# Sparse attention and a two-layer MLP on one core: the order of the first loads and the filler products at the start

## The chip, the core and the metric

The kernel runs on one core of a Trainium2 chip. A core has five engines that each work through an instruction stream of their own: TensorE (PE, the matrix products; its weight loads are listed apart as PEld), VectorE (DVE), ScalarE (ACT), GpSimd (POOL) and SyncE (SP). DMAs are issued from the streams of SP, ACT and POOL and travel on queues that belong to the issuing engine. The metric is the device time in microseconds (us) of one launch; lower is better. Several runs are made and the median is taken.

## The reference

The computation is a block of sparse attention followed by a two-layer network. q, k and v are float32 of shape 8 x 8 x 576 x 64 (batch, head, sequence, head dimension).

```
scores = scale * q @ k^T                                   # per batch and head
mask   = local  (0 <= row-col < 32)                        # heads 0 to 3
       | strided (row >= col and row % 32 == col % 32)     # heads 4 to 7
attn   = softmax(where(mask, scores, -1e9)) @ v
x      = attn, heads side by side: (8*576) x 512
h      = x @ w_in                                          # 512 -> 2048
g      = max(h, 0) + alpha * min(h, 0)
out    = g @ w_out                                         # 2048 -> 512, float32
```

## The kernel before

The heads of one batch make two units: the four local heads and the four strided heads. Unit 0 is local and unit 1 strided for batch 0, units 2 and 3 are those of batch 1, and so on. Two heads form a pair, and a pair's work is cut into pieces: `T` transposes q or k of a unit on TensorE (line 248) and copies the result to SBUF; `Sc` makes scores (L350), adds the mask with one more product (L366) and takes the exponential on ScalarE (L371, L374); `Pv` multiplies by v (L451), and VectorE divides by the row sums (L458, L460); `X` transposes the attention output into `xT` (L468).

The network takes 512 rows of x at a time. `lin1_piece` multiplies by w_in (L633), followed by a ReLU on ScalarE (L643) and an add on VectorE (L646); `lin2_piece` (L660), or `lin2_sums` from the third block on (L750), multiplies by w_out. There are nine such blocks. Attention of batch 0 runs alone at the start; everything after it interleaves attention pieces of later batches with the network's pieces.

Nothing is planned at run time: every call is wrapped in `keep`, and each engine executes its own instructions in the order in which the program emits them. That order matters most at the start, in the code from line 811 on:

- `load_qk(0, True, "q")` and `load_qk(0, True, "k")` (L123) load q and k of the four strided heads of batch 0, 512 KB each in float32. q goes by SP's queue and k by ACT's. Between the two calls the identity matrix, the first 128 columns of `consts` (32 KB), is issued on SP (L825). The rest of `consts` (90 KB, the masks, L832) and alpha (L833) follow on SP.
- VectorE has memsets: `wrm`, which the filler products read (L820), the padding of two buffers (L822) and of `x16s` (L823), then more (L842 to L845).
- POOL issues, in this order, the strided tails (`tl`, L158), the local q and k of batch 0 (`ql`, `kl`, L123), the local tails (L162), v for the strided heads (`stv`, L172), v for the local heads (`vl`, L180), then the four chunks of w_in (L801), of w_out (L797) and the loads of batch 1.
- `warm(n)` (L805) emits n filler products of 128x128 by 128x512 into a bank that nobody reads (L808). Twelve come first; then, in the loop over the pieces of batch 0, eight stand behind piece 0 (the transposes of q), three behind piece 1 (the transposes of k and of the tails), and one behind many of the later pieces.
- `id16` (L862) copies a corner of the identity; it needs the identity to have landed. Then `cast_s` casts q to float16, both halves on VectorE, and k, one half on VectorE (L190) and one on ScalarE (L188). `madd` (L865) makes the additive mask from the second part of `consts`.
- Piece 0 then transposes q, and copies its two halves from PSUM to `qT`, the first on VectorE (L190) and the second on ScalarE (L188). Piece 1 transposes k (one half copied on ScalarE, one on VectorE) and the tails (L273).
- At piece 4, VectorE casts v of the strided heads (`vs`).

Of the kernel before, what the change touches and what calls it, by code (L numbers as in the profile page):

```python
# [31 lines left out]
def kernel(  # L32
# [10 lines left out]
    nc = tc.nc  # L43
    keep = tc.keep_in_program_order
# [55 lines left out]
    x16s = cpool.tile([80, 1024], F16)  # L100
    qks = {nm: cpool.tile([80, 4, 512], F16, name=f"{nm}sd") for nm in "qk"}
# [5 lines left out]
    def load_qk(b, strided, nm):  # L107

        h0 = 4 if strided else 0
        src = q if nm == "q" else k
        if strided and b:
            t16 = hpool.tile([128, 2, 512], F16, tag=f"{nm}s", bufs=2, name=f"{nm}s")
            cast16[(b, True, nm)] = t16
        else:
            t16 = hpool.tile([128, 2, 512], F32, tag=f"{nm}l", bufs=2, name=f"{nm}l")
            loaded[(b, strided, nm)] = t16
        base = src[b, h0 : h0 + 1, 0:1, :]
        eng = nc.sync if (b > 2 and not strided) or (b == 0 and strided) else nc.gpsimd  # L120
        if b == 0 and strided and nm == "k":
            eng = nc.scalar
        keep(eng.dma_start(t16, bass.AP(  # L123
            tensor=base.tensor, offset=base.offset,
            ap=[[8 * D, 64], [2 * S * D, 2], [S * D, 2], [1, 8 * D]])))
# [13 lines left out]
    def cast_s(b, nm, eng):  # L139
        t16 = hpool.tile([128, 2, 512], F16, tag=f"{nm}s", bufs=2, name=f"{nm}s")  # L140
        if eng[0] == eng[1]:
            cast_copy(eng[0], t16, loaded[(b, True, nm)])
        else:
            for f in range(2):
                cast_copy(eng[f], t16[:, f : f + 1, :], loaded[(b, True, nm)][:, f : f + 1, :])
        cast16[(b, True, nm)] = t16
# [39 lines left out]
    def cast_copy(eng, o, i):  # L186
        if eng == "act":
            keep(nc.scalar.copy(o, i))  # L188
        elif eng == "dve":
            keep(nc.vector.tensor_copy(o, i))  # L190
        else:
            keep(nc.gpsimd.tensor_copy(o, i))

    def cast_v(b, pr, eng):

        v16 = vss[b % 2]
        cast_copy(eng, v16[0:72, 2 * pr : 2 * pr + 2, :, 0:64],
                  loaded[b][0:72, 1024 * pr : 1024 * pr + 1024].rearrange(
                      "p (h t d) -> p h t d", h=2, t=8))
        cast16[(b, True, "v")] = v16  # L200
# [338 lines left out]
    for g in range(7, npair + 2):  # L539
# [30 lines left out]
        for i, (kind, fn) in enumerate(seq):  # L570
# [6 lines left out]
            def run(fn=fn, extra=extra, g=g, c=c, kind=kind, lastp=(i == lastP), first=(i == 0)):  # L577
                fn()
                for b, pr in extra:
                    if pr in ("q", "k"):  # L580
                        cast_l(b, pr)
                        if b + 1 < B:
                            load_qk(b + 1, False, pr)
                        continue
                    cast_v(b, pr, "pool")
                    if pr == 1 and b + 1 < B:
                        load_v(b + 1, True)
                if kind == "Tk" and g % 4 == 3 and c + 3 < B:
                    load_tail(c + 3, False)
                if lastp:  # L590
                    if 4 * DX <= g - 1 < npair and pairs[g - 1].xd:
                        x_dma(pairs[g - 1])
                    if g % 4 == 3 and DX <= c + 1 < B:
                        transpose_d()
                    if g % 4 == 2 and DX <= c and c + 1 < B:
                        load_d(c + 1)
                    if g % 4 == 1 and DX < c and c + 1 < B:
                        load_v(c + 1, False)
                if first and 4 * DX <= g - 3 < npair and pairs[g - 3].xd and pairs[g - 3].strided:
                    x_copy(pairs[g - 3])  # L600
# [10 lines left out]
    def attn_step(end):  # L611
        if pos["i"] < end:
            pieces[pos["i"]][1]()
            pos["i"] += 1
        while late:
            late.pop(0)()
        if defer:
            defer.pop(0)()
# [186 lines left out]
    def warm(n):  # L805

        for _ in range(n):
            keep(nc.tensor.matmul(wps, wrm[:, 0:128], wrm, start=True, stop=True))  # L808


    wrm = gsum[0].rearrange("p k c -> p (k c)")[:, 0:512]
    wps = banks[2]
    def load_unit(b, strided, v_too=True):
        load_qk(b, strided, "q")
        load_qk(b, strided, "k")
        load_tail(b, strided)
        if v_too:
            load_v(b, strided)

    keep(nc.vector.memset(wrm, 0.0))  # L820
    for nm in "qk":
        keep(nc.vector.memset(qks[nm][64:80], 0.0))  # L822
    keep(nc.vector.memset(x16s[64:80], 0.0))  # L823
    load_qk(0, True, "q")
    keep(nc.sync.dma_start(consts[:, 0:128], consts_dram[:, 0:128]))  # L825
    load_qk(0, True, "k")
# [2 lines left out]
            name=nc.get_next_instruction_name(), act_func_set_id=6, ins=[], outs=[]  # L829
        )  # L830
    ))
    keep(nc.sync.dma_start(consts[:, 128:488], consts_dram[:, 128:488]))  # L832
    keep(nc.sync.dma_start(alpha_r, moe_alpha.rearrange("(kf p) -> kf p", p=128)))  # L833
    load_tail(0, True)
# [25 lines left out]

    warm(12)
    keep(nc.vector.tensor_copy(id16, ident[0:16, 0:16]))  # L862
    cast_s(0, "q", ("dve", "dve"))
    cast_s(0, "k", ("dve", "act"))
    keep(nc.vector.tensor_scalar(  # L865
        madd, consts[:, 128:488], -1.0, 30000.0, op0=ALU.add, op1=ALU.mult))
# [1 line left out]
    for i in range(end0):  # L868
        if i == 6:
            keep(nc.tensor.transpose(apt[:, 0:16], alpha_r, id16))  # L870
            keep(nc.vector.tensor_scalar(
                oma, apt[:, 0:16], -1.0, 1.0, op0=ALU.mult, op1=ALU.add))
        if i == 4:
            cast_v(0, 0, "dve")
            cast_v(0, 1, "dve")
        attn_step(end0)
        if i < 2:
            warm((8, 3)[i])
        elif i not in (2, 3, 4, 5, 11, 12, 14, 16):
            warm(1)  # L880

# [90 lines left out]
```

## Time and profile before

| quantity | value |
|---|---|
| median of 7 runs | 316.08 us (314.43 to 316.84) |
| time of the profiled execution | 316.84 us |
| span of the profiled execution, first to last instruction | 315.0 us |
| PE busy | 302.7 us, 96% of the span |
| DVE / ACT / POOL busy | 221.1 / 178.5 / 168.4 us |
| first `lin1_piece` product begins | 26.90 us |
| first score product begins | 13.71 us |
| mean DMA rate | 128 GB/s over the span |

In the rows below, a line of the timeline gives the start and the duration in us, the engine, the line of the kernel, the operation, what it writes and reads, how many were merged, and in brackets how long the engine stood idle before it and what ended that wait. "SPq" and "ACTq" are DMAs being issued by those engines. The chain is the list of work that ended last, followed backward from the end: for each piece its start, its length and what it was.

### The profile page before, as it was taken

How to read it: one execution, taken by the hardware profiler on the slowest of the kernel's cores; microseconds unless marked ns; L12 is line 12 of the kernel's file. 1: busy time of each engine (PE TensorE's matmuls, PEld its weight loads, DVE VectorE, ACT ScalarE, POOL GpSimd, SP SyncE). 2: the span in 40 equal slices, each digit the busy share in tenths (PEclk: the TensorE clock that was granted, in tenths of full speed). 3: DMA queues.
4: the chain of work that ended last, by engine and by line, in shares of the span. 5: the costliest groups of instructions: out<-in, count | busy, mean ns of one | idle time of the engine just before them, and what ended most of it. 6: DMA issues, size and time to landing. Idle time of an engine off the chain costs nothing.

```text
span 315.0 us, 7067 instructions
## 1 busy us (share of the span) xinstructions
PE 302.7 (96%) x2808; PEld 193.8 (62%) x2808; DVE 221.1 (70%) x408; ACT 178.5 (57%) x331; POOL 168.4 (53%) x175
## 2 busy tenths in 40 slices
PE   5999989999999999999999999999999999999995
PEld 1465445554454448844888888448844784585484
DVE  4466888457823789578856885689568967855872
ACT  2375645469566776476647754775467426615630
POOL 8672399235969773967396729672726301201300
PEclk9799999999999999999999999999999999999999
DMA  7999999999699992899699929963920040002003
GB/s 226 185 206 207 212 208 181 186 140 248 127 144 161 255 94 31 120 280 127 61 184 255 93 45 177 156 60 50 173 85 6 16 123 33 2 33 102 0 3 133
DMA packets 81202, 40.38 MB, mean 128 GB/s; under 512 B 58625, under 2 KB 76305, under 8 KB 81169
## 3 DMA queue, kind: packets, MB, share of 16 engines
q0 software_dynamic: 41728, 17.38, 50.2%
q1 hardware_dynamic: 39168, 22.03, 31.1%
q10 hardware_dynamic: 272, 0.52, 0.5%
q8 instruction: 22, 0.36, 0.5%
q14 instruction: 12, 0.09, 0.1%
HBM read 38.01 MB, written 9.44 MB: 151 GB/s over the span
## 4 chain that ended last, share of the span: by engine, by line
PE 64%; DVE 14%; ACT 8%; issue 4%; POOL 4%; DMA 4%; SPq 0%; ACTq 0%; DVEq 0%
PE hb L633 25%; PE hb L750 20%; PE hb L660 6%; DVE gT L646 6%; PE pv L451 3%; DVE x L460 2%; ACT neg L643 2%; PE tp L248 2%; DMA kl<-in_k_dram 2%; DVE wsum L690 2%; PE hb L808 2%; DMA consts<-consts 2%; ACT xT L490 2%; ACT et L421 2%; PE sp L408 1%
## 5 line engine op out<-in xcount | busy, mean ns | idle before, releaser
L646 DVE SCALAR_TENSOR_TENSOR gT<-neg,oma,hb 128x512 f16<-128x512 f32 x144 | 105.3, 744 | 40.4 <-ACT neg L643 33.7
L633 PE MATMUL hb<-xT,win 128*128 128x512 f16 (+1 forms) x640 | 132.9, 358 | 0.7
L643 ACT ACTIVATE neg<-hb 128x512 f32<-128x512 f32 x144 | 86.0, 597 | 39.2 <-PE hb L633 37.8
L633 PEld LDWEIGHTS <-win 128*128 128x128 f16 x640 | 60.1, 98 | 56.3 <-issue 2.6
L423 POOL TENSOR_TENSOR et<-et,consts 128x576 f16<-128x576 f16 (+1 forms) x24 | 30.6, 1276 | 54.4 <-ACT et L421 50.9
L702 POOL TENSOR_TENSOR gsum<-gT 128x512 f16<-128x512 f16 x21 | 24.2, 1150 | 50.6 <-DVE gT L646 50.6
L750 PEld LDWEIGHTS <-gsum 128*128 128x128 f16 x448 | 41.3, 98 | 5.9 <-DVE gsum L702 1.1
L750 PEld LDWEIGHTS <-gT 128*128 128x128 f16 x336 | 31.4, 98 | 6.8 <-DVE gT L646 1.8
L460 DVE TENSOR_TENSOR x<-pv,rc 96x384 f16<-96x384 f32 (+2 forms) x62 | 33.0, 532 | 2.1
L660 PE MATMUL hb<-wout,gT 128*128 128x512 f16 x128 | 32.5, 379 | 0.6 <-ACT osb L665 0.5
L430 POOL TENSOR_TENSOR et<-et,consts 128x576 f16<-128x576 f16 (+1 forms) x24 | 30.6, 1276 | 0.6 <-ACT et L427 0.6
L762 ACT COPY o<-hb 128x512 f32<-128x512 f32 (+1 forms) x28 | 15.8, 564 | 26.4 <-PE hb L750 26.4
L451 PEld LDWEIGHTS <-et 72*128 72x128 f16 (+1 forms) x448 | 23.7, 98 | 9.4 <-POOL et L430 0.9
L750 PE MATMUL hb<-wout,gT 128*128 128x256 f16 x216 | 28.0, 273 | 0.7 <-DVE gT L646 0.4
L458 DVE RECIPROCAL rc<-pv 72x6 f32<-72x6 f32 (+2 forms) x80 | 14.6, 183 | 19.0 <-PE pv L451 18.6
L750 PE MATMUL hb<-wout,gsum 128*128 128x256 f16 x216 | 26.9, 273 | 0.2 <-DVE gsum L702 0.2
L750 PE MATMUL hb<-wsum,gsum 128*128 128x256 f16 x216 | 26.3, 272 | 0.2 <-DVE gsum L702 0.2
L421 ACT ACTIVATE et<-sp 128x576 f16<-128x576 f32 (+1 forms) x24 | 15.5, 645 | 19.2 <-PE sp L408 19.2
L765 DVE TENSOR_TENSOR o<-hb,o 128x512 f32<-128x512 f32 (+1 forms) x21 | 14.2, 677 | 14.3 <-PE hb L750 10.6
L427 ACT ACTIVATE et<-sph 128x288 f16<-128x288 f32 (+1 forms) x48 | 18.4, 410 | 0.0
L188 ACT COPY qT<-tp 128x1024 f16<-128x1024 f16 (+1 forms) x11 | 8.9, 819 | 15.4 <-DVE qT L190 10.1
L660 PEld LDWEIGHTS <-gT 128*128 128x128 f16 x128 | 11.0, 97 | 9.8 <-issue 0.7
(104 smaller groups left out, 337.0 us busy)
## 6 DMA issues: line engine op xcount, KB each, us to landing
out_dram<-o SPq DMA_DIRECT2D x27, 256.0 KB, 3.0
ql<-in_q_dram SPq DMA_DIRECT2D x6, 512.0 KB, 6.1
kl<-in_k_dram SPq DMA_DIRECT2D x5, 512.0 KB, 7.0
stv<-in_v_dram POOLq DMA_DIRECT2D x8, 288.0 KB, 6.6
vl<-in_v_dram POOLq DMA_DIRECT2D x6, 384.0 KB, 8.2
win<-in_moe_w_in_dram POOLq DMA_DIRECT2D x4, 512.0 KB, 11.3
wout<-in_moe_w_out_dram POOLq DMA_DIRECT2D x4, 512.0 KB, 13.2
out_dram<-osb SPq DMA_DIRECT2D x8, 256.0 KB, 5.4
```

The source lines that it names most:

```text
L421: keep(nc.scalar.activation(ev.rearrange("r (y c) -> r y c", y=2), sp[0:r, :, 0:n], AF.Exp, scale=SCALE))
L423: keep(nc.gpsimd.tensor_tensor(mv, mv, m, op=ALU.mult))
L427: keep(nc.scalar.activation(ev[:, n * y : n * y + n], sps[y][0:r, 0:n], AF.Exp, scale=SCALE))
L430: keep(nc.gpsimd.tensor_tensor(mv, mv, m, op=ALU.mult))
L451: keep(nc.tensor.matmul(pv[:, 65 * x : 65 * x + 65], et[0:r, c : c + 128], v16[0:r, 2 * P.pr + hh, t, :] if P.strided else v16[:, 6 * (2 * ...
L460: keep(nc.vector.tensor_tensor(P.x16[0:w, c0 : c0 + 64 * nb].rearrange("r (c e) -> r c e", e=64), pvv[:, :, 0:64], rc[0:w, 0:nb].unsqueeze ...
L633: keep(nc.tensor.matmul(hps[:, dst : dst + w], win16[:, kk, 128 * m : 128 * m + 128], xT[:, kk, src : src + w], start=(kk == 0 and x == 0) ...
L643: keep(nc.scalar.activation(neg, hps, AF.Relu, scale=-1.0))
L646: keep(nc.vector.scalar_tensor_tensor(gTs[n][:, m, :], neg, oma[:, m : m + 1], hps, op0=ALU.mult, op1=ALU.add))
L660: keep(nc.tensor.matmul(ops, gTs[n][:, kf, 128 * mt : 128 * mt + 128], wout16[:, kf, :], start=(kf == 0), stop=(kf == 15)))
L702: keep(eng.tensor_tensor(o[:, k0:k1], x[:, k0:k1], y[:, k0:k1], op=op))
L750: keep(nc.tensor.matmul(dst, lhs[:, kf, 128 * mt : 128 * mt + 128], rhs[:, kf, :], start=(first and own and kf == 0), stop=(kf == 7), skip ...
```

## The change

q of the strided heads of batch 0 goes by ACT's queue and k by SP's; since the identity is emitted between the two calls, SP now issues the identity first and k second. The four memsets of L820 to L823 move behind the load of ScalarE's function table in the program. The second half of the q cast goes to ScalarE. Behind each of the first two pieces stand four filler products, where there were eight and three.

```diff
-        if b == 0 and strided and nm == "k":
+        if b == 0 and strided and nm == "q":
             eng = nc.scalar
@@
-    keep(nc.vector.memset(wrm, 0.0))
-    for nm in "qk":
-        keep(nc.vector.memset(qks[nm][64:80], 0.0))
-    keep(nc.vector.memset(x16s[64:80], 0.0))
     load_qk(0, True, "q")
     keep(nc.sync.dma_start(consts[:, 0:128], consts_dram[:, 0:128]))
     load_qk(0, True, "k")
     keep(nc.scalar.add_instruction(
         mybir.InstLoadActFuncSet(
             name=nc.get_next_instruction_name(), act_func_set_id=6, ins=[], outs=[]
         )
     ))
+    keep(nc.vector.memset(wrm, 0.0))
+    for nm in "qk":
+        keep(nc.vector.memset(qks[nm][64:80], 0.0))
+    keep(nc.vector.memset(x16s[64:80], 0.0))
     keep(nc.sync.dma_start(consts[:, 128:488], consts_dram[:, 128:488]))
@@
-    cast_s(0, "q", ("dve", "dve"))
+    cast_s(0, "q", ("dve", "act"))
     cast_s(0, "k", ("dve", "act"))
@@
         attn_step(end0)
         if i < 2:
-            warm((8, 3)[i])
+            warm(4)
         elif i not in (2, 3, 4, 5, 11, 12, 14, 16):
             warm(1)
```

## The prediction

> **What bounds the kernel now.** The page says PE is busy 96% of the span, so a change confined to the first microseconds can only move when PE's long work begins. I read the chain that ended last, in order of time, for the head:
>
> ```profile
> 1.53 5.58 DMA consts<-consts
> 7.11 0.02 issue
> 7.13 0.55 DVE id L862
> 7.68 0.54 DVE qs L190
> 8.23 0.05 issue
> 8.27 1.02 PE tp L248 x8
> 9.30 3.00 PE hb L808 x8
> 12.29 0.45 PE tp L248 x8
> ...
> 27.39 13.77 PE hb L633 x63
> ```
>
> The head waits for the identity until 7.11 us, runs the q transposes, and then lets eight fillers (L808) stand for 3.00 us before the k transposes. Next, when the two big loads land (KB, then us from issue to landing):
>
> ```profile
> ql<-in_q_dram SPq DMA_DIRECT2D x1, 512.0 KB, 5.9
> kl<-in_k_dram ACTq DMA_DIRECT2D x1, 512.0 KB, 4.4
> consts<-consts SPq DMA_DIRECT2D x1, 32.0 KB, 5.6
> ```
>
> Issued at 0.73, 0.74 and 1.53 us: q is there at 6.6, k at 5.1, and the identity, behind q on SP's queue, at 7.1. Then the timeline up to the first score product:
>
> ```profile
> 9.34 0.69 DVE L190 COPY qT<-tp 128x512 f16<-128x512 f16 x1 [0.43 <-PE tp L248]
> 10.06 0.58 ACT L188 COPY qT<-tp 128x512 f16<-128x512 f16 x1 [4.31 <-DVE qT L190]
> 12.78 0.58 ACT L188 COPY kT<-tp 128x512 f16<-128x512 f16 x1 [2.13 <-PE tp L248]
> 13.44 0.33 ACT L188 COPY kT<-tt 128x64 f16<-128x64 f16 x2
> 13.71 0.30 PE L350 MATMUL sp<-qT,kT 64*128 64x72 f16 x8
> ```
>
> The second qT copy waits for the first (10.03 to 10.06), and the scores start at 13.71, when the first k tail is copied. Last, the granted clock (the figure before the DMA share):
>
> ```profile
> 7.50:8.00 0.50, 0.00 (x0) 0.00 (x0) 0.50 (x2) 0.00 (x0) 0.50 (x2) 1.00 1.06 401
> 8.50:9.00 0.50, 0.50 (x8) 0.50 (x6) 0.40 (x2) 0.00 (x0) 0.21 (x2) 0.50 1.00 377
> 12.00:12.50 0.50, 0.50 (x9) 0.38 (x8) 0.00 (x0) 0.00 (x0) 0.50 (x2) 1.00 2.39 165
> ```
>
> After PE stood idle from 5.77 to 8.27 the clock was at half from about 8.33 to 11.74; that is why eight fillers took 3.00 us, where a filler behind them takes 0.22.
>
> **The change, part by part.**
>
> *The identity.* It is issued at 0.73 as SP's first DMA, with nothing ahead of it on its queue. `id16` then runs when VectorE's memsets end (4.50, row L845) and no longer ends a wait.
>
> *q on ACT's queue.* k took 4.4 there from the same issue time: q lands at 0.74 + 4.4 = 5.1. Its halves are cast side by side, 0.60 on DVE and 0.62 on ACT (the rows of the two k halves), done at 5.75. By the rows the halving itself buys nothing (q's whole cast took 0.54, 7.68 to 8.22, on the chain; one k half takes 0.60); it adds 0.62 to ACT, which stands idle until k lands anyway. ACT's table load stays behind one 512 KB issue, as before. The twelve fillers end at 5.77, so the q transposes start at about 5.85 instead of 8.27, and PE hardly idles.
>
> *k on SP's queue.* It is now SP's second issue, which in this trace starts at 1.53. Nearest row: SP's 512 KB took 5.9 beside the same load on ACT's queue, so k lands at 7.4. Here a rule stands against the row. The Trainium skill, "DMA: Bandwidth & Descriptors", section "Issuing engines are not separate DMA queues", says that DMAs of all engines run on the same 16 DMA engines and interleave, and the issuing engine only saves issue time. By it q and k share evenly and, with the same bytes to move, the pair is complete when it was before, 6.6: k would be 0.8 earlier. The rows show two equal loads issued within 0.01 us landing 1.5 apart, so queues do differ; I take 7.4. Ends: 5.9 (1.53 + ACT's 4.4) and 8.2 (1.53 + the 6.7 of POOL's 512 KB load of local k).
>
> *What is queued behind k.* This is the step that decides. Both halves of the k cast stand on DVE and ACT ahead of the qT copies, and `madd` too, whose masks follow k on SP (they came 0.9 after q before, so about 8.0 now, just when the k cast ends). So q, though early, waits for k. From k's landing: cast 0.62, `madd` 0.23, qT on DVE 0.69, qT on ACT 0.58, kT on ACT 0.58, first tail 0.27 (13.44 to 13.71), handovers about 0.2: 3.17 together. Scores start at 7.4 + 3.17 = 10.57 instead of 13.71: **3.1 us earlier**.
>
> *Fillers.* Four behind q: at full clock 4 x 0.216 = 0.9, at half 1.7; from 5.85 + 0.85 of transposes that is over by 7.6 to 8.4. k's weights are ready at 8.0, so at most 0.4 of it shows at the k transposes, and that lies under the qT copies that run until about 9.5. Four behind k cost 0.9 from about 8.9 at full clock, over before 10.57: hidden. All at half clock, 8.0 + 0.9 + 0.3 + 1.7 = 10.9: 0.3 would show. If the copies were gone, the four behind q would cost 0.4 and those behind k 0.9.
>
> *The clock*, the second rule. The Trainium skill, "TensorE: Matmul & The Clock Gate", Part 4, says that transposes do not count as PE-busy for the clock; Part 1, that the clock is decided over windows of some 3.4 us. The trace agrees on the window (8.33 to 11.74 is 3.41). With fillers alone counted, PE would be busy 0.85 + 0.9 of the 3.41 from 4.92 to 8.33, about half, where 0.85 alone (before) brought half clock. By the rule, half clock could come back until 11.74: the 0.3 above, plus half of the score work from 10.9 to 11.74, 0.4. The sum would be 2.4 earlier instead of 3.1. I take 3.1, since half a window filled is a different case from a quarter, and keep 2.4.
>
> *Memsets.* They move only against instructions of other engines; on DVE their order is the same, and they end at 4.50, before q lands. They pass only ACT's and SP's issues and the table load. No cost; a late `wrm` (0.86 now) would delay only the first fillers.
>
> **Can the rest follow 3.1 us earlier?** Loads on POOL's queue are not moved, so I compare landing and first use. v of the strided heads: issued 5.74, 6.8 to landing, 12.5, then 0.42 per cast on DVE, 12.9 (13.3 for both); first used at 16.44. Beyond 3.1 to 3.5 it becomes the wait, which caps the gain and brings the early end of k (5.9) to no more than 3.5. Local v copy ends 18.03, used 22.77: room 4.7. w_in's last chunk: landed 25.8, used 26.9 + 12 x 0.864 = 37.3: 11.5. Batch 1's strided q: 20.91 + 16.4 = 37.3, used 43.36: 6.0; k 5.2; its local k cast ends 48.06, used 52.78: 4.7. Later loads are issued behind work that moves too. So the whole is 3.1 earlier.
>
> **The sum.** Profiled execution: span 315.0 - 3.1 = 311.9, time 316.84 - 3.1 = 313.7. The median lies 0.76 below that execution: 316.08 - 3.1 = 313.0. Part of the 0.76 may be the clock's window falling better around the old fillers, a luck that the new head needs less, so I take the middle, **313.3**.
>
> **Rivals.**
> 1. *k is late or half clock returns.* k at 8.2 leaves 2.3, half clock 2.4: 313.3 + 0.8 = 314.1, with both 314.8. For it: k now overlaps POOL's local loads more. Against: PE's near-gapless start.
> 2. *The gain is hidden.* If a fixed load later sets the pace, nothing is left: 316.1. For it: DMA is over-full from 9 us on, about 206 GB/s until 35. Against: the smallest room I found after the first v is 4.7. It would also be the case if the first v, not cast until 13.3, were later by 3.
> 3. *Slower: k starves on SP.* One mechanism: POOL's local q and k (1 MB, issued 3.07 and 3.79) are served ahead of k, as ACT's load was served ahead of SP's. They land at 8.8 and 10.5; k could come about 1.7 after them, 12.2. Each us of k beyond 10.5 (13.71 - 3.17) costs one us, so it decides from there: 12.2 gives 316.1 + 1.7 = 317.8. Against: SP's q landed 2.2 before POOL's first.
>
> **How the numbers follow.** A measurement of this kernel can tell about 0.5% (1.6 us) from no change. Chances: forecast 0.66; rival 1 0.16; rival 2 0.10; rival 3 0.08. Faster (below 314.5) holds nearly all of the forecast (0.63) and half of rival 1: 0.71. Slower is rival 3, 0.08, and the rest, 0.21, is the same. The range runs from 312.0 (3.5 off the median, and 0.6 for its scatter) to 316.2, which takes in rivals 1 and 2; outside it are rival 3 and about 0.07 below.
>
> **What would show it.** `id16` no longer waits for the identity; q transposes at about 5.9; k lands near 7.4, and ACT and DVE wait for that load; the qT copies begin right behind the k cast and `madd`, not behind the transposes; first score at 10.6; first L633 product at 23.8; PEclk 1.00 after some 8 us. Wrong if k lands after 9, if the first pv waits for v's cast, if the clock drops to 0.50 again, or if PE shows a DMA wait between 24 and 60.

## The result and the profile after

The changed kernel takes 313.71 us (median of 26 runs, 312.44 to 317.15), beside 316.04 us for the kernel before in the same session (63 runs, 314.4 to 317.77): a ratio of 0.993, 95% interval 0.9915 to 0.9946. That is 2.33 us, or 0.7%, less. The profiled execution took 313.75 us with a span of 311.9 us. One thing is needed to read these medians: in the sessions of the experiments, the runs of the kernel before whose mean granted clock is 1.00 (38 of 118) take 314.4 us in the median, and those at 0.995 or less 316.0 to 316.5 us; of the changed kernel's runs (the profiled one included) 20 of 27 are at 1.00, with a median of 313.3, and the other seven have 314.3.

The timeline of the changed kernel, up to the first product of the network (start, us, engine, line, operation):

```profile
0.74 0.70 ACTq L123 DMA_DIRECT2D ql<-in_q_dram  x1
0.74 0.34 SPq L821 DMA_DIRECT2D consts<-consts  x1
...
1.14 0.78 SPq L123 DMA_DIRECT2D kl<-in_k_dram  x1
...
4.42 0.13 DVE L862 CAST id<-consts 16x16 f32<-16x16 f16 x1
...
5.19 0.62 ACT L188 CAST qs<-ql 128x512 f16<-128x512 f32 x1 [2.44 <-DMA ql<-in_q_dram]
...
5.71 0.72 PE L248 MATMUL tp<-consts,qs 128*128 128x128 f16 x8
...
6.50 1.19 POOL L180 DMA_DIRECT2D vl<-in_v_dram  x1
6.88 0.62 ACT L188 CAST ks<-kl 128x512 f16<-128x512 f32 x1 [1.07 <-DMA kl<-in_k_dram]
6.88 1.06 DVE L190 CAST ks<-kl 128x512 f16<-128x512 f32 x1 [1.26 <-DMA kl<-in_k_dram]
...
7.87 0.23 DVE L865 TENSOR_SCALAR madd<-consts 128x360 f16<-128x360 f16 x1
...
8.00 0.62 PE L248 MATMUL tp<-consts,ks 128*128 128x128 f16 x8 [0.70 <-DVE ks L190]
8.02 0.68 DVE L190 COPY qT<-tp 128x512 f16<-128x512 f16 x1
...
8.73 0.58 ACT L188 COPY qT<-tp 128x512 f16<-128x512 f16 x1 [1.24 <-DVE qT L190]
...
9.98 0.30 PE L350 MATMUL sp<-qT,kT 64*128 64x72 f16 x8 [0.17 <-ACT kT L188]
...
12.99 0.76 DVE L190 COPY vs<-stv 72x1024 f16<-72x1024 f16 x2 [2.46 <-DMA stv<-in_v_dram]
13.47 0.36 PE L451 MATMUL pv<-vs,et 72*128 72x65 f16 x6 [0.70 <-DVE vs L190]
```

The identity's copy no longer waits. Instead ACT and DVE wait for k, which lands at about 6.85; `madd` and then the qT copies follow right behind the k cast. Scores begin at 9.98 instead of 13.71, but the first product with v then waits 0.70 us, because v, whose load was not moved, lands at 12.96. Of the 3.73 us by which the scores are earlier, 2.97 are left at 13.47. The first product of the network begins at 23.93 instead of 26.90, and the last product of the kernel ends 3.1 us earlier (307.40 instead of 310.48).

The loads issued in the first 8 us of the changed kernel (KB, then us from issue to landing):

```profile
ql<-in_q_dram ACTq DMA_DIRECT2D x1, 512.0 KB, 4.4
kl<-in_k_dram SPq DMA_DIRECT2D x1, 512.0 KB, 5.7
...
consts<-consts SPq DMA_DIRECT2D x1, 32.0 KB, 1.7
```

The identity takes 1.7 us where it took 5.6 behind q, and SP's 512 KB are again slower than ACT's. The granted clock, in windows of the changed kernel (the column ahead of the DMA share):

```profile
7.50:8.00 0.50, 0.00 (x0) 0.00 (x1) 0.50 (x2) 0.00 (x0) 0.50 (x2) 1.00 1.11 320
...
8.50:9.00 0.50, 0.50 (x8) 0.28 (x6) 0.32 (x2) 0.27 (x1) 0.24 (x1) 1.00 1.00 364
```

It stays at 1.00, where the kernel before had 0.50 in the second of these windows.

Between 43 and 50 us, part of the lead is lost once more: by comparison of the same products, it is 3.53 us at the scores of 43.22 (46.75 before) and 2.94 at the transposes of 50.54 (53.48 before). There VectorE sums w_out (L690) beside POOL's casts of batch 1. After:

```profile
39.51 1.22 DVE L690 TENSOR_TENSOR wsum<-wout 128x2048 f16<-128x2048 f16 x1
...
42.20 2.02 POOL L192 COPY vs<-stv 72x1024 f16<-72x1024 f16 x2
...
43.69 4.89 DVE L690 TENSOR_TENSOR wsum<-wout,wsum 128x2048 f16<-128x2048 f16 x2
```

The kernel before has its first sum here, stretched, since it meets POOL's copy of v:

```profile
41.78 2.02 POOL L192 COPY vs<-stv 72x1024 f16<-72x1024 f16 x2
42.48 2.39 DVE L690 TENSOR_TENSOR wsum<-wout 128x2048 f16<-128x2048 f16 x1
43.74 2.03 POOL L192 CAST ql<-ql 128x1024 f16<-128x1024 f32 x1
```

The first sum takes 1.22 us beside POOL's issue of a DMA (39.54) and about twice that beside POOL's copies. In the changed kernel it finishes before the copies begin, which is why the lead has grown from 2.97 to 3.53; the next two sums meet the casts instead. Which of two overlapping instructions is drawn out can go either way; in two clear pairs it is the one that began second. Without fillers (below) a sum begun at 46.52 took 1.22 and the cast that POOL began at 46.56 took 2.08 instead of 1.07; with eight more fillers (below) the cast, begun at 46.09, took 1.07 and the sum, begun at 46.21, 2.04.

### The profile page after: what moved, and what is told of

Its sections match the earlier page's. It is cut to its first block, busy times and chain, and to the rows that moved or that the text cites. A ratio compares the mean times of both kernels' runs of the same rounds, so it can differ in the third digit from the quotient of the medians.

```text
span 311.9 us, 7063 instructions
## 1 busy us (share of the span) xinstructions
PE 300.8 (96%) x2805; PEld 192.8 (62%) x2805; DVE 220.5 (71%) x408; ACT 178.9 (57%) x332; POOL 167.3 (54%) x175
## 4 chain that ended last, share of the span: by engine, by line
PE 52%; DMA 16%; DVE 12%; POOL 9%; ACT 7%; issue 4%; ACTq 0%; POOLq 0%; DVEq 0%
PE hb L633 19%; PE hb L750 18%; DMA kl<-in_k_dram 8%; PE hb L660 6%; DVE gT L646 5%; DMA wout<-in_moe_w_out_dram 5%; DMA vl<-in_v_dram 3%; DVE x L460 2%; ACT et L421 2%; POOL vs L192 2%; PE pv L451 2%; PE tp L248 2%; POOL et L430 2%; POOL et L423 2%; DVE wsum L690 2%
## 5 line engine op out<-in xcount | busy, mean ns | idle before, releaser
L646 DVE SCALAR_TENSOR_TENSOR gT<-neg,oma,hb 128x512 f16<-128x512 f32 x144 | 105.3, 744 | 40.3 <-ACT neg L643 33.5
L427 ACT ACTIVATE et<-sph 128x288 f16<-128x288 f32 (+1 forms) x48 | 18.4, 410 | 0.0
```

The lines of the kernel that those rows point to most:

```text
L427: keep(nc.scalar.activation(ev[:, n * y : n * y + n], sps[y][0:r, 0:n], AF.Exp, scale=SCALE))
L646: keep(nc.vector.scalar_tensor_tensor(gTs[n][:, m, :], neg, oma[:, m : m + 1], hps, op0=ALU.mult, op1=ALU.add))
```

## The experiments

The expectations name these theories. A, as the prediction has it: the gain is the earlier start that q, k and the identity get by their queues; what caps it is v, then whatever comes later. B: the gain is that fewer fillers stand between the transposes. C: the gain is the clock that no longer drops. D, for the later runs: VectorE's sums beside POOL's casts hold the work up a second time. All times are beside runs of the kernel before on the same chip.

**The exchange of q and k alone.** The kernel before with one word changed; memsets, q cast and fillers are as before.

```diff
-        if b == 0 and strided and nm == "k":
+        if b == 0 and strided and nm == "q":
```

> The change's loads alone (strided q on ACT's queue; identity, then k on SP's), with q cast whole on VectorE and eight and three fillers as before. Theory A (the identity and q arrive early, the q transposes start at about 5.8 while the clock is still full, and the k transposes then wait for k): eight fillers at full clock take 1.7, the k transposes start at 8.2 to 8.6 instead of 8.0, the first score product at 10.0 to 10.4, the first product with v still at about 13.5 because v lands at 13.0; median 313.6 to 314.1. Theory B (the fewer fillers between the transposes of q and of k are the gain): at most 1 us is left, 315.0 or more.

Measured 313.3 us (312.85 to 313.63) beside 316.02, ratio 0.9911 (0.9888 to 0.9934). All six runs are at clock 1.00. Scores start at 9.82, and both figures are a little better than expected. So the exchange alone gives all of the gain; memsets, q cast and fillers add nothing that can be seen. (Six runs are too few to tell its odds of a full clock from those of the whole change.) Its trace also shows which instruction pays beside POOL's issue of v's load:

```profile
6.57 1.32 POOL L180 DMA_DIRECT2D vl<-in_v_dram  x1
6.67 0.62 ACT L188 CAST ks<-kl 128x512 f16<-128x512 f32 x1 [3.92 <-DMA kl<-in_k_dram]
6.67 0.43 DVE L190 CAST ks<-kl 128x512 f16<-128x512 f32 x1 [0.98 <-DMA kl<-in_k_dram]
7.04 0.91 DVE L865 TENSOR_SCALAR madd<-consts 128x360 f16<-128x360 f16 x1
```

Here k's half is cast in 0.43 and `madd` takes 0.91 instead of 0.23, ending as POOL's issue ends (7.89); in the changed kernel the cast is the stretched one, 1.06, and ends at 7.94, with POOL's issue over at 7.69. The cast here lies wholly within POOL's issue too and is not stretched, so standing beside the issue is not enough by itself.

**The fillers alone**, in the kernel before.

```diff
-            warm((8, 3)[i])
+            warm(4)
```

> The change's fillers alone (four and four), loads and casts as before. Theory A: the q transposes stay at 8.3 and, the clock at half, four fillers fewer let the k transposes start 1.5 to 1.7 earlier, at about 10.6; first score product at 12.1 to 12.4, first product with v at about 15.0; median 314.5 to 314.8. Theory B: most of the change, 313.7 to 314.2. Theory C (the clock is the gain; TensorE's idle time before the q transposes stays, so half clock does): 315.7 to 316.1.

Measured 315.03 us (313.69 to 316.5), ratio 0.9971 (0.995 to 0.9992). Nine of the 18 runs are at full clock (median 314.2), nine below (315.87), where the kernel before had 8 of 28 at full clock. That lies between what A and C expected. Fewer fillers change the odds of the clock, and shorten the head a little (k transposes at 9.57 in the profiled run, which was at full clock, where the next kernel, also at full clock, has 10.44). It is part of a gain, but not one that adds to the first: the exchange alone was already as fast as the whole change.

**Only the clock.** The kernel before, with eight more fillers ahead of the q transposes, so that TensorE is busy while it waits for the identity.

```diff
-    warm(12)
+    warm(20)
```

> The kernel before with 20 instead of 12 fillers ahead of the q transposes, so that TensorE is busy until about 7.5 and not only until 5.8; nothing else. Theory A: q transposes still at 8.3, since the identity still lands at 7.1; the clock stays full, eight fillers take 1.7 instead of 3.0, the k transposes start about 1.6 earlier; median 314.4 with nearly all runs near the lower bunch of the times before (314.4 to 314.5). Theory C (the clock is the whole gain): 313.7. If half clock was never what made the times before scatter: 316.0 with the same scatter.

Measured 314.4 us (314.37 to 314.72), ratio 0.9952 (0.9932 to 0.9973), every run at full clock. Loads, casts and the order are those of before:

```profile
8.26 0.62 PE L248 MATMUL tp<-consts,qs 128*128 128x128 f16 x8 [0.92 <-DVE qs L190]
...
8.71 1.89 PE L808 MATMUL hb<-gsum 128*128 128x512 f16 x8
```

This is what theory A expected. The q transposes start when they did (8.27 before), and the row of the eight fillers has 1.89 where the same row has 3.20 before (3.00 on the chain). So the clock alone is worth 1.6 us, and the earlier head a further 1.1, the difference of the medians at full clock, 314.4 - 313.3. The traces agree: at the first product with v this kernel stands 1.69 ahead of before (14.75), the changed one 2.97, which is 1.28 more. Neither A nor C alone was the whole.

**k ahead of the identity on SP**, in the changed kernel.

```diff
-    keep(nc.sync.dma_start(consts[:, 0:128], consts_dram[:, 0:128]))
     load_qk(0, True, "k")
+    keep(nc.sync.dma_start(consts[:, 0:128], consts_dram[:, 0:128]))
```

> The changed kernel with k first and the identity second on SP. Theory A (the identity's landing sets the q transposes, because its copy stands on VectorE ahead of the casts): k lands at about 6.6, the identity at about 7.1, the q transposes start at 8.2, TensorE idles before them, the clock falls to half in many runs, and the kernel is near the one with the change's fillers alone: median 314.6 to 315.2. Rival (only q and k matter, and k is earlier): 313.5 or less.

Measured 315.33 us (313.26 to 316.71), ratio 1.0002 (0.9975 to 1.0029): nothing of the gain is left in the median, and 4 of the 14 runs are at full clock.

```profile
7.14 0.54 DVE L862 CAST id<-consts 16x16 f32<-16x16 f16 x1 [2.64 <-DMA consts<-consts]
...
8.01 1.03 PE L248 MATMUL tp<-consts,qs 128*128 128x128 f16 x8 [2.60 <-DVE qs L190]
...
8.83 1.92 PE L808 MATMUL hb<-gsum 128*128 128x512 f16 x4
```

k lands at 6.64, a little earlier than in the changed kernel, but the 32 KB identity needs 5.6 us behind it, TensorE idles 2.60 us, and four fillers then take 1.92. The clock was at half from about 7.6 to 11.0. So the exchange gains nothing without the identity's early place, and k's landing was not the point. What the place gives by itself, the next run shows.

**q and k as before, only the identity ahead.** The changed kernel with k on ACT's queue, and on SP the identity, then q.

```diff
-        if b == 0 and strided and nm == "q":
+        if b == 0 and strided and nm == "k":
@@
-    load_qk(0, True, "q")
     keep(nc.sync.dma_start(consts[:, 0:128], consts_dram[:, 0:128]))
+    load_qk(0, True, "q")
     load_qk(0, True, "k")
```

> The changed kernel with the two big loads exchanged between the queues: identity, then q on SP, k on ACT. Theory A (the order in which the pieces land decides, and the casts stand in the order q, k on both engines): k lands at about 5.1 and q at about 6.9, both casts follow q, the q transposes start at 7.6 to 8.0 and the four fillers stand between them and the k transposes, so these start at 9.0 to 9.5 at full clock and later at half; scores from 10.9 to 12; median 313.9 to 315. Rival (all queues share the same engines, so which queue carries which does not matter): as the changed kernel, 313.7.

Measured 314.69 us (313.06 to 317.05, 22 runs), ratio 0.9951 (0.9934 to 0.9969); 13 runs at full clock, median 314.12.

```profile
kl<-in_k_dram ACTq DMA_DIRECT2D x1, 512.0 KB, 4.2
ql<-in_q_dram SPq DMA_DIRECT2D x1, 512.0 KB, 5.4
```

The slower load goes with the queue and not with the tensor; whether the queue makes it, or the smaller loads that SP's queue carries besides, was not separated. The q transposes begin at 7.08, 1.4 later than in the changed kernel; the k transposes at 8.53, not at the 9.0 or later that was expected, the scores at 10.26, and v is waited for (13.39). The identity's place alone thus gives most of the gain, 1.58 us of the median where the changed kernel has 2.06 on that chip. At full clock, though, that kernel has a median of 313.07, a microsecond less. Part of an answer stands in the traces, whose spans are alike, 312.4 for this one and for the changed kernel there (an execution of 314.21, the slowest of its runs at full clock). In both, TensorE waits at 97.9 us (1.44 and 1.42), because the transposing DMA of attention output (`xs`, L483) lands 6.4 and 6.3 us after its issue; with the exchange alone it took 4.1 and in the first trace of the changed kernel 3.2, and TensorE waited 0.16. Why that DMA is late in some executions, and how often, stays open, and with it the microsecond between the medians.

**No fillers behind the first two pieces**, in the changed kernel.

```diff
-            warm(4)
+            pass
```

> The changed kernel with no fillers behind the first two pieces. Theory A: the k transposes still start at 8.0 and the scores at 10.0, since k's landing and the copies set them; but TensorE then idles from about 6.3 to 8.0 and from 8.8 to 10.0, and the clock falls to half in most runs (granted clock 0.995 or less): median 314.2 to 315. Rival (the four fillers still cost time): 313.4 or less.

Measured 316.05 us (314.38 to 318.17, 22 runs), ratio 1.0016 (0.9995 to 1.0037); no run at full clock. The windows of its trace:

```profile
8.00:9.00 1.00, 0.03 (x2) 0.00 (x0) 0.71 (x3) 0.52 (x2) 1.00 (x2) 1.00 0.95 346
9.00:10.00 1.00, 0.27 (x9) 0.22 (x10) 0.41 (x1) 0.79 (x4) 1.00 (x2) 1.00 1.61 198
...
11.00:12.00 1.00, 0.88 (x11) 0.41 (x10) 0.00 (x0) 0.66 (x3) 1.00 (x2) 0.50 1.78 171
...
16.00:17.60 1.60, 1.60 (x14) 1.32 (x13) 0.78 (x3) 0.64 (x3) 0.74 (x1) 0.50 1.24 206
```

k's transposes (7.06) and the scores (9.73) come even earlier than with fillers, but TensorE is idle nearly all the time between 8.0 and 9.7, and the clock is at half from about 10.8 to 17.6. At the first product with v the lead over before is still 3.2, at the scores of the local heads behind it 1.4 (18.00 beside 19.38), and at the first product of the network 1.4 (25.51 beside 26.90). It was expected at 314.2 to 315: half clock costs more than that, since it lasts twice as long here and lies over attention products, not over fillers as before. The traced execution, 314.62, is one of the quicker ones; seven of the 22 have a mean clock of 0.982 to 0.984, lower than its 0.989. The fillers' own time was not on the path; the clock that they hold up is.

**The old fillers, eight and three**, in the changed kernel.

```diff
-            warm(4)
+            warm((8, 3)[i])
```

> The changed kernel with eight and three fillers as before. Theory A (fillers are hidden behind k's landing and the copies; eight rather than four close the idle stretch before the k transposes and keep the clock at full): the start of the scores stays within 0.2 of 10.0, no run with the clock at 0.995, times like those of the loads alone: median 313.2 to 313.4. Theory B (fewer fillers are a gain in themselves): 314.3 or more.

Measured 313.12 us (312.73 to 314.48, 15 runs), ratio 0.9951 (0.9932 to 0.997). Ten runs at full clock (312.95), five at a lower one (314.38). The k transposes are at 8.00 and the scores at 9.98, as with four and four: eight fillers behind q fit in the wait for k. So fewer fillers were no gain. Nor do more of them keep the clock at full in every run, which had been expected.

**v of the strided heads first on POOL**, in the changed kernel.

```diff
+    load_v(0, True)
     load_qk(0, False, "q")
@@
-    load_v(0, True)
     load_v(0, False)
```

> The changed kernel with the load of v for the strided heads moved ahead of the local q and k on POOL's queue. Theory A (after the change the landing of v, 13.0, sets the first product with v): v lands at about 10, the first product with v starts at 12.7 instead of 13.5, 0.75 earlier, and the local q and k, 0.7 later, are still in time; span 311.2, median 312.9 to 313.1. Rival (the room is used up by the later loads or by local q and k): 313.6 or more.

Measured 313.69 us (312.48 to 315.4, 9 runs), ratio 0.993 (0.99 to 0.9959): no gain over the changed kernel, as the rival had it. The first product with v does come 0.76 earlier (12.71), and the network starts at 23.16. But at 49.4 TensorE waits for POOL's cast of k, and the lead over the changed kernel is 0.04:

```profile
42.92 5.55 DVE L690 TENSOR_TENSOR wsum<-wout,wsum 128x2048 f16<-128x2048 f16 x2
44.21 2.03 POOL L192 CAST ql<-ql 128x1024 f16<-128x1024 f32 x1
...
47.46 1.90 POOL L192 CAST kl<-kl 128x1024 f16<-128x1024 f32 x1
```

Both casts, and two sums that take 5.55 us instead of 2 x 1.22, are drawn out where they overlap. The v wait was a real cap, and behind it stands a second one.

**The sums moved away**: in the changed kernel, three sums behind pieces 12, 13 and 14 of the block instead of 1, 3 and 5.

```diff
-        if i in (1, 3, 5):
-            w_sums(nc.vector, ({1: 1, 3: 2, 5: 4}[i],))
+        if i in (12, 13, 14):
+            w_sums(nc.vector, ({12: 1, 13: 2, 14: 4}[i],))
```

> The changed kernel with the three sums of w_out blocks (L690 on VectorE) made after pieces 12, 13 and 14 of the first block's second product instead of after pieces 1, 3 and 5. Theory D (after the head there is a second gate: in the changed kernel the last two sums ran 4.89 us, 43.7 to 48.6, beside GpSimd's casts of batch 1, where 1.22 each is what one takes alone, and VectorE's copies behind them hold TensorE at 50.5): each sum takes 1.2 to 1.3, TensorE is 0.6 earlier at the tail transposes of batch 1, span about 311.3, median 313.0 to 313.2 with less scatter. Rival (VectorE just has that work to do, wherever it stands): 313.6 or more.

Measured 315.31 us (313.3 to 317.89, 14 runs), ratio 0.9992 (0.9964 to 1.002). Each sum now takes 1.21, and at 50 us TensorE is 0.89 ahead of the changed kernel (0.26 of it from an earlier head in this execution). By 63 us all of it is given back:

```profile
59.16 1.21 DVE L690 TENSOR_TENSOR wsum<-wout,wsum 128x2048 f16<-128x2048 f16 x1
61.12 0.30 PE L468 MATMUL xp<-consts,x 96*128 96x96 f16 x3 [0.34 <-DVE x L460]
61.68 1.21 DVE L690 TENSOR_TENSOR wsum<-wout,wsum 128x2048 f16<-128x2048 f16 x1
61.81 0.30 PE L468 MATMUL xp<-consts,x 96*128 96x96 f16 x3 [0.39 <-DVE x L460]
62.81 0.45 DVE L190 COPY xT<-xp 128x576 f16<-128x576 f16 x1
```

The second sum stands on DVE ahead of two divisions of attention output (`x`, 60.51 and 61.20), for which TensorE waits, and the third ahead of the copy of `xT` that the network's next block reads. The stretching is real; moving the work merely moves who waits for it. The rival was right. The median is also one of more half clock: seven of the 14 runs are below full, and those at full have 313.94.

**v first, with eight and three fillers.** Both edits shown above together, in the changed kernel.

> The changed kernel with eight and three fillers and v of the strided heads loaded ahead of the local q and k. Theory D (the three sums on VectorE beside GpSimd's casts are a second gate whose end does not move with the head): the first product with v is 0.7 earlier than with eight and three fillers alone, and nearly all of it is gone at the tail transposes of batch 1; median 312.9 to 313.2. Rival (no second gate): 312.3 to 312.5.

Measured 312.74 us (312.43 to 313.71) beside 316.27 on that chip, ratio 0.9897 (0.9864 to 0.9929), every run at a clock of 0.998 or more. The head is not shorter (scores at 10.15), but v is cast by 12.25, and the product with v starts at 12.88. This is the lowest median of the study, 1.0% under the kernel before. Against the changed kernel on the same chip, 314.21 us (17 runs, below), the difference is mostly the clock: at full clock that one takes 313.07. The median lies between the two forecasts. The traces speak for theory D: beside eight and three fillers alone this one is 0.32 earlier at the first product with v (13.20 there) and 0.08 at the tail transposes of batch 1 (49.55 and 49.63).

**The same with the sums moved into the second block's first layer**, behind its pieces 1, 4 and 7.

```diff
-        if i in (1, 3, 5):
-            w_sums(nc.vector, ({1: 1, 3: 2, 5: 4}[i],))
@@
                     lin1_piece(n, i)
+                    if i in (1, 4, 7):
+                        w_sums(nc.vector, ({1: 1, 4: 2, 7: 4}[i],))
```

> As the one before, and the three sums moved to pieces 1, 4 and 7 of the second block's first product, where GpSimd stood idle for 7.9 us and VectorE is half idle. Theory D: the sums take 1.2 to 1.3 each and hold nothing up, so what v's earlier landing gives stays: span 310.2 to 310.6, median 312.1 to 312.5. Rival (VectorE just has that work to do, as when the sums stood late in the first block): 313.1 or more.

Measured 313.66 us (313.34 to 314.03), ratio 0.9922 (0.9894 to 0.9951): 0.9 slower than without the move, as the rival had it. It is 1.39 ahead of the changed kernel at 49 us and 0.09 at 74:

```profile
70.47 1.27 POOL L423 TENSOR_TENSOR et<-et,consts 128x576 f16<-128x576 f16 x1 [8.32 <-ACT et L421]
70.56 2.25 DVE L690 TENSOR_TENSOR wsum<-wout,wsum 128x2048 f16<-128x2048 f16 x1
73.53 0.81 PE L633 MATMUL hb<-xT,win 128*128 128x512 f16 x3 [0.85 <-DVE gT L646]
```

Two of the sums took 1.22, but the third began as POOL came back to work and took 2.25; VectorE's add for the first layer (L646) came late behind it, and TensorE waited for that.

**The changed kernel again**, beside the last three.

> The changed kernel itself, on the same chip as the three before it. Both theories: 313.4 to 314.0, first score product at 9.7 to 10.1, first product with v 0.4 to 0.5 after v lands.

Measured 314.21 us (312.31 to 316.69, 17 runs) beside 316.27, ratio 0.9941 (0.9916 to 0.9966), above the 313.4 to 314.0 expected; nine runs at full clock (313.07), eight below (315.23). The share of runs that keep their clock is thus not the same on every chip, 20 of 27 on the first and 9 of 17 here. Its trace has the same head (scores 10.11, first v product 13.44), leads the first trace by 0.66 at 50 us and stands 0.49 behind it at 97 us, when attention output is transposed. Its waits there, 45 to 100 us, have the late DMA named above:

```profile
PE xp L468 <- ACT et L427: 1.4, 1, 1.4
ACT xT L490 <- DMA xs<-x16s: 1.1, 1, 1.1
```

ACT's exponentials (L427) stand behind its copy of `xT`, which waits for that DMA, and TensorE waits for them.

## Why the prediction was right, step by step

313.3 us was forecast and 313.71 measured, for the reason given: the head begins earlier and the later work follows. For the profiled execution, the sum gave a span of 311.9 and 313.7 us; it has 311.9 and 313.75. That agreement is luck in good part, since several of the steps were off and compensate.

- **Identity and q: as forecast.** `id16` at 4.42 (4.5), q's casts from 5.19 (5.1), its transposes at 5.71 (5.85). The identity's place on SP decides: without it the gain is gone.
- **k's landing: 6.85, not 7.4.** The row for the duration held (5.7 for 5.9); the issue time did not. The sum took 1.53 from a trace where the first DMA of SP is a 512 KB load, but the identity's issue keeps SP for 0.34 only, and k goes out at 1.14. The evenly shared queue of the rule weighed there would have given 6.6, which is nearer; but the durations, 4.4 and 5.7, and 4.2 and 5.4 with the tensors exchanged, are not those of an even share.
- **From k to the scores: 3.13, forecast 3.17**, but not by its own terms. DVE's half of the k cast took 1.06 instead of 0.60. (That 0.60 was itself a row beside an issue of POOL's; alone the half takes 0.43, as q's does here at 5.20.) The Trainium skill, "SBUF — State Buffer", section "Who interferes with whom", says that VectorE in its two-port modes and GpSimd lock each other out of a shared pair of ports for a whole instruction. VectorE's stretched instruction ends near the end of POOL's issue of v's load (7.94 and 7.69 here, 7.95 and 7.89 with the exchange alone, 7.86 and 7.81 without fillers), which would fit a lock in its last part; a cast of 0.43 within the same issue (6.67, with the exchange alone) does not fit one over its whole length, and no run isolates it. Cast and `madd` together reached from 6.85 to 8.02, 1.17 where 0.85 was counted. That was made up by ACT's copies, which begin 0.49 and 0.47 after the one ahead where 0.58 each was counted, and by the 0.2 for handovers, which was not needed.
- **Scores: 3.73 earlier, forecast 3.1**, by the earlier k. Here one of the forecast's own signs of being wrong came true: the first product with v waits for v's cast. v was counted as landing at 12.5 and landed at 12.96; TensorE waited 0.70, and 2.97 is left. So the early k and the late v cancel, which the forecast did not foresee, though v was named as the cap.
- **Fillers "hidden": right for their own time, wrong for their worth.** Four or eight behind q make no difference to the scores. But a return of half clock was sized at 0.7 us. In the changed kernel its runs below full clock are 1.0 us longer on the first chip (314.26 beside 313.29) and 2.2 on the last (315.23 beside 313.07); without fillers, when it lasts from 10.8 to 17.6, nothing of the gain is left.
- **The clock.** The trace after shows 1.00, as taken. The rival with half clock is not void, though: 7 of 27 runs are below full. Whether transposes count as busy for the clock, which the second rule denies, no run here separates. The forecast's 3.1 us contain the half clock of the profiled execution, whose eight fillers stand in it at 3.00; what is left against a run at full clock it did not say. At full clock the kernel before takes 314.4, and the head is worth 1.1 beside that. By the medians, 1.6 us are the clock, 1.1 the head, and 0.4 is given back, since not all runs of the changed kernel keep the full clock (316.04 - 1.6 - 1.1 + 0.4 = 313.7).
- **The middle between the two bases of the sum** (316.84 and the median) came out near the mark, but not for the reason offered. Both lie among the runs at 0.995 (315.6 to 317.3 on one chip), so the 0.76 between them is not full clock against half; what it is, no run shows.
- **"The smallest room I found after the first v is 4.7": failed.** It was found by landings and first uses. Between 43 and 50 us the limit is not a landing but VectorE and POOL in each other's way, and 0.59 of the lead goes there (and 0.73 more when v comes earlier). The whole still ended 3.1 earlier because the lead going in was 3.53. A wait of TensorE for a DMA between 24 and 60, the sign named for this, is not in the trace.
- **Memsets and q's halves**: no effect seen, as forecast, the exchange without either being as fast. Two readings on the way were off. q's whole cast was taken as 0.54, which is only its part on the chain; its row has 1.00 there and 0.69 with the exchange alone, so a half does save some 0.26, hidden behind the wait for k. And masks that land 0.9 after a k at 7.4 come at 8.3 and not 8.0; they landed at 7.17 and were not waited for.

## What to carry to other kernels

Put a small load that gates the first work ahead of the large ones on its queue, and cost a head by what it does to the granted clock as well as by its length: a gap of 2.5 us near the start cost 1.6 us more than its length here, in the median, although fillers already stood on both sides of it. When a head is shortened, look for the next landing and then for two engines that slow each other down where they newly overlap; room between a landing and its use doesn't show those. And split the runs by granted clock before reading a median of this size: two kernels can differ by their odds of a full clock rather than by their work.

## What the runs showed of the hardware

- Two 512 KB loads issued within 0.4 us of each other land 4.1 to 4.6 us after issue on ACT's queue and 5.4 to 6.1 on SP's, whichever tensor each carries; a 32 KB load takes 1.7 to 1.8 us as SP's first and 5.3 to 5.8 behind 512 KB.
- The identity's issue keeps SP for 0.34 us when it is SP's first and 0.82 to 0.83 when it is the second; a 512 KB load's issue takes 0.74 to 0.75 as the first and 0.77 to 0.78 as the second.
- One idle stretch of 2.5 us on TensorE, at the start, was followed by half clock for 3.41 us; one of about 1.7 us (8.0 to 9.7, without fillers) by half clock for 6.8. Another of 1.76 us (four and four fillers in the kernel before) was not, in the traced execution, and nine of that kernel's 18 runs are below full clock. So the length of the gap alone does not decide.
- VectorE's sums of 128x2048 took 1.21 to 1.22 us beside POOL's DMA issues or nothing, and up to 3.09 (5.55 for two) beside POOL's copies and casts; where the sum began first, it kept its 1.22 and POOL's cast took 2.08. A `madd` of 0.23 took 0.91 beside a POOL DMA issue.
- The same transposing DMA (`xs`, L483) landed 3.2 to 6.4 us after its issue in the traces of these kernels, and from 5.6 on ACT waited for it (0.41 to 1.17).
